# Other start addresses for the on-chip tiles of a convolution and feed-forward kernel

## The chip, the cores and the metric

The kernel runs on one core of a Trainium2 chip. The metric is the device time of one execution in microseconds (us): 2256.51 before the change, the median of 3 runs (2256.26 to 2256.53). The engines named below are TensorE (PE in the profile, with its weight loads as PEld), VectorE (DVE), ScalarE (ACT), GpSimd (POOL) and SyncE (SP, which here only issues transfers). SBUF is the on-chip memory of 128 partitions; an address below is a byte within a partition, the same one in all partitions. PSUM is the memory into which TensorE writes.

## The reference

A causal convolution of 7 taps, with softmax weights per head, feeds a two-layer network. x is [8, 4096, 192], the weights are w_in [192, 2048] and w_out [2048, 192], all in float32.

```python
w = exp(weight - max); w = w / (sum(w) + 1e-9)             # [8 heads, 7 taps]
x_unf = x_pad[:, idx, :].reshape(B, S, K, H, group)
conv = np.einsum('hk,bskhg->bshg', w, x_unf).reshape(B*S, D)
h = conv @ w_in
g = np.where(h >= 1, h, np.where(h <= -1, 0, (h + 1)**2 / 4))
out = g @ w_out
```

## The kernel before

**Tiling.** The 32768 tokens are cut into 64 blocks of 512, and the 2048 hidden columns into 16 chunks of 128, taken two at a time: 8 steps a block, 512 steps in all, each for one block `s` and one pair of chunks `j`. In a step, `mm1` computes the hidden values h of this step, and `mm2` adds the product of the values of two steps earlier to the sums of the output. Between the two, DVE clips h (L458), ACT squares (L464), DVE takes the maximum with h (L469), ACT rounds to a high part `gh` (L476), and DVE subtracts to get the low part `gl` (L482).

**Matmuls.** From the second block on, each factor is split into a high and a low part (type float32r), and three of the four products are computed. A matmul here takes 64 of the 128 rows of the array, and two of them, one on the upper and one on the lower 64 partitions, run side by side: a "pair" below. Each has 64x128 weights (one LDWEIGHTS) and a moving operand of 64x512 values, 2048 consecutive bytes in each partition. `mm1` (L407) is 9 such pairs in a step, with the weights from `W` (tile names w0 to w9) and the convolution's output (hi, lo, rh, rl, rhi, rlo) as the moving operand. `mm2` (L447) is 10 pairs, with weights from `W` and `WR` (wr) and gh or gl as the moving operand.

**The first block** is different: there `mm1` takes plain float32 (fp32) operands, with w_in's values `WI`, which lie in tiles of the names gh and gl, as weights, and the convolution's tiles as the moving operand. `mm2_first` (L425), for the first two blocks' sums, takes g as weights and `WF` (wf, 192 columns) as the moving operand. In the profile each fp32 matmul is recorded as two.

**Convolution.** For each two blocks, three tiles of x are loaded (raw), transposed on DVE (xT), multiplied by a tap's weight on ACT (p), and summed on GpSimd (y). Then y is split into hi and lo, and copies with the halves of the partitions exchanged are made by DMA (hi<-hi, lo<-lo and so on). `PLAN_A`, `PLAN_B` and `PLAN_R` set the step in which each part is issued; for example, the b tile is split in step 5 and first read by `mm1` in step 8. The very first unit of the convolution is summed on TensorE from xT (L190), with taps that start at `xT[.., SH + k]`, SH = 26 values.

**Order.** The schedule is written by hand (`manual_schedule`): each engine takes its instructions in the order of the program text, and each instruction waits on semaphores for what it reads.

**Addresses.** SBUF tiles are laid out from byte 16512 up, pool by pool in the order in which the pools are opened (L72 to L78), and within a pool in the order of first use; each tile takes its size rounded up to 32 bytes. Before the change that gives:

- const: W from 16512 (128 past a multiple of 1024), then WR, WF, wk, warm, whose, ident, up to 79680. W, WR and WF have sizes that are multiples of 512, and a matmul's 128 weights of 512 bytes start at multiples of 512 in them, so every weight load from them starts 128 past a multiple of 512.
- stage, 33792 bytes (33 times 1024).
- xin and xw (raw, xT, y, p), 21120 bytes, from 113472.
- xo, act, ob (hi, lo, rh, ..., gh, gl, g, sum, osb, t) from 134592. All of these tiles have 2048 or 4096 bytes, so all start 448 past a multiple of 1024, and 1472 past a multiple of 2048.

Of the kernel before, what the change touches and what calls it, by code (L numbers as in the profile page):

```python
# [8 lines left out]
F32 = mybir.dt.float32  # L9
# [9 lines left out]
P = 128  # L19
# [11 lines left out]
def lightconv_then_ffn(ctx: ExitStack, tc: tile.TileContext, x, weight, w_in, w_out, out):  # L31
# [26 lines left out]
    H, K = weight.shape  # L58
# [12 lines left out]

    const = ctx.enter_context(tc.tile_pool(name="const", bufs=1))  # L72
    stage = ctx.enter_context(tc.tile_pool(name="stage", bufs=2))
    xin = ctx.enter_context(tc.tile_pool(name="xin", bufs=3))
    xw = ctx.enter_context(tc.tile_pool(name="xw", bufs=2))
    xo = ctx.enter_context(tc.tile_pool(name="xo", bufs=3))
    act = ctx.enter_context(tc.tile_pool(name="act", bufs=2))
    ob = ctx.enter_context(tc.tile_pool(name="ob", bufs=2))  # L78
    ps_h = ctx.enter_context(tc.tile_pool(name="ps_h", bufs=2, space=PSUM))
    ps_o = ctx.enter_context(tc.tile_pool(name="ps_o", bufs=1, space=PSUM))  # L80
    ctx.enter_context(tc.manual_schedule())
# [53 lines left out]
    class Conv:  # L135
# [133 lines left out]
        def split_halves(self):  # L269
# [26 lines left out]
    wo_w = w_out.bitcast(U32).rearrange("(f p) (d two) -> p f d two", p=P, two=2)  # L296
    n_in = [CI if j < NPAIR else 0 for j in range(NCH)]
    n_all = [n_in[j] + (CO if j >= LAG else 0) for j in range(NCH)]
    W = [const.tile([P, 2, n_in[j] + (CW if j >= LAG else 0)], F32R, name=f"w{j}")
         for j in range(NCH)]  # L300
    CC = max(n_all)
# [12 lines left out]
    class Chunk:  # L314
# [51 lines left out]
        def parts(self, rest):  # L366
            j, k = self.j, n_in[self.j]
            if rest:
                yield (WF[j][:, :, 0:P],
                       *(W[j][:, i, k:].rearrange("p (f d) -> p f d", f=2) for i in range(2)))  # L370
                yield WF[j][:, :, P:], WR[j][:, :, 0], WR[j][:, :, 1]
            else:
                yield WI[j], W[j][:, 0, 0:k], W[j][:, 1, 0:k]

# [14 lines left out]
    def mm1(q):  # L389
# [11 lines left out]
        else:  # L401
            mms = [(W[j][:, part], u + u, [xop[s][u, x]] * 2) for u in "nsr"
                   for part, x in ((0, "hi"), (1, "hi"), (0, "lo"))]
# [25 lines left out]
    def mm2(q):  # L429

        s, j = divmod(q, NPAIR)
        gh, gl = ghs.pop(q), gls.pop(q)
        w, wr, k = W[j + LAG], WR[j + LAG], n_in[j + LAG]
        if j == 0:
# [97 lines left out]
    def evac_last(s):  # L532
# [29 lines left out]
                    in_=y[i][:, 0:2 * D].rearrange("p (b d) -> p b d", b=2))  # L562


    wk = const.tile([P, 2, K], F32, name="wk")
    warm = const.tile([P, 1], F32, name="warm")
    whose = const.tile([P, 2 * P + 3 * K + 3], F32, name="whose")[:, 0:2 * P]
    one = ob.tile([P, TB], F32, name="sum")[:, 0:P]
    small, busy = (ob.tile([P, TB // SQ, SQ], F32, name="osb").rearrange("p j b -> p (j b)")
                    for _ in range(2))  # L570
    wmax, wsum, wk2, rows = (small[:, i:i + n] for i, n in (
        (0, 1), (1, 1), (2, K), (2 + K, K)))
    ident = const.tile([P, P], F32, name="ident")


    KD = (("a", 0), ("r", 1), ("r", 3), ("r", 5), ("r", K - 1))
# [331 lines left out]
```

## Time and profile before

| | us |
|---|---|
| median of 3 runs (2256.26 to 2256.53) | 2256.51 |
| span of the profiled execution, first to last instruction | 2256.3 |
| ACT busy in it | 1697.6 (75%) |
| POOL busy in it | 1168.5 (52%) |
| DMA read from and written to HBM | 32.84 MB and 25.17 MB, 26 GB/s |

The profiled execution's own time is known by its span, and 2256.3 us lies within the three measured runs; nothing measurable stands around it. "Busy" of TensorE is the union of matmul durations, and these overlap, so a busy TensorE can still be waiting inside its pipeline; what tells is the distance from one matmul's start to the next. The chain of waits is followed back from the last instruction, at each step to what released it.

### The profile page before, as it was taken

The numbers are of one execution on the slowest core, as the hardware profiler recorded it, in microseconds if no ns is written. First come the engines' busy times: TensorE is split into PE (matmuls) and PEld (weight loads), VectorE is DVE, ScalarE is ACT, GpSimd is POOL, SyncE is SP. The second block draws the span as 40 slices with busy tenths as digits, with TensorE's granted clock in tenths as the row PEclk, the third lists the DMA queues.
The fourth block names the chain that finished last, engine by engine and source line by source line (L and its number), as shares of the span: only waits on it lengthen the run. The fifth ranks groups of instructions, "written<-read, shape, count | busy, mean of one in ns | idle before, by whom it ended". The sixth has DMA issues, their size and how long they took to land.

```text
span 2256.3 us, 48204 instructions
## 1 busy us (share of the span) xinstructions
PE 2250.8 (100%) x19646; PEld 2232.0 (99%) x19646; DVE 2103.4 (93%) x1883; ACT 1697.6 (75%) x2153; POOL 1168.5 (52%) x868
## 2 busy tenths in 40 slices
PE   9999999999999999999999999999999999999999
PEld 6999999999999999999999999999999999999999
DVE  8899999999999999999999999999999999999997
ACT  7677877778777787777877777877778777787775
POOL 1546644556445565454654455644556545565441
PEclk9999999999999999999999999999999999999999
DMA  7222222222222212222222222222222222212211
GB/s 158 49 51 46 43 44 49 51 52 39 52 48 46 53 35 51 49 49 51 39 47 47 49 51 49 40 48 45 50 53 39 51 49 46 54 34 51 49 34 24
DMA packets 442125, 110.84 MB, mean 49 GB/s; under 512 B 410288, under 2 KB 417840, under 8 KB 441904
## 3 DMA queue, kind: packets, MB, share of 16 engines
q1 hardware_dynamic: 441744, 107.66, 25.8%
q8 instruction: 155, 2.54, 0.5%
q14 instruction: 66, 0.54, 0.1%
q10 hardware_dynamic: 160, 0.10, 0.0%
HBM read 32.84 MB, written 25.17 MB: 26 GB/s over the span
## 4 chain that ended last, share of the span: by engine, by line
PE 100%; DMA 0%; DVE 0%; ACT 0%; issue 0%; DVEq 0%
PE h L407 47%; PE accm L447 30%; PE accr L447 20%; PE accr L425 1%; PE accm L425 1%; PE accr L190 0%; PE accr L407 0%; PE accm L175 0%; DMA osb<-in_weight_dram 0%; PE h L155 0%; PE accm L181 0%; PE accr L641 0%; PE h L548 0%; PE accm L407 0%; PE accr L548 0%
## 5 line engine op out<-in xcount | busy, mean ns | idle before, releaser
L230 POOL TENSOR_TENSOR y<-y,p 128x512 f32<-128x512 f32 x546 | 765.5, 1402 | 729.4 <-DVE g L469 558.6
L482 DVE TENSOR_TENSOR gl<-g,gh 128x1024 fp32r<-128x1024 f32 (+1 forms) x497 | 732.4, 1474 | 27.5 <-ACT gh L476 23.7
L407 PE MATMUL h<-hi,w 64*128 64x512 f32 x4032 | 740.6, 389 | 0.0
L464 ACT ACTIVATE g<-g 128x1024 f32<-128x1024 f32 (+1 forms) x505 | 535.2, 1060 | 241.8 <-DVE g L458 232.4
L476 ACT CAST gh<-g 128x1024 fp32r<-128x1024 f32 (+1 forms) x497 | 521.7, 1050 | 237.2 <-DVE g L469 223.6
L458 DVE TENSOR_SCALAR g<-h 128x1024 f32<-128x1024 f32 (+1 forms) x505 | 609.7, 1208 | 96.5 <-PE h L407 88.4
L469 DVE TENSOR_TENSOR g<-h,g 128x1024 f32<-128x1024 f32 (+1 forms) x505 | 613.6, 1215 | 11.9 <-ACT g L464 4.5
L447 PE MATMUL accm<-gh,w 64*128 64x512 f32 x3968 | 614.4, 388 | 0.0
L407 PEld LDWEIGHTS h<-hi,w 64*128 64x128 f32 x4032 | 580.3, 184 | 0.0
L407 PE MATMUL h<-lo,w 64*128 64x512 f32 x2016 | 555.9, 388 | 0.0
L447 PEld LDWEIGHTS accm<-gh,w 64*128 64x128 f32 x3968 | 513.1, 184 | 0.0
L447 PE MATMUL accr<-gh,wr 64*128 64x512 f32 x1984 | 387.3, 388 | 0.0
L447 PE MATMUL accm<-gl,w 64*128 64x512 f32 x1984 | 387.3, 388 | 0.0
L447 PE MATMUL accr<-gl,wr 64*128 64x512 f32 x1984 | 387.3, 388 | 0.0
L219 ACT ACTIVATE p<-xT,wk 128x512 f32<-128x512 f32 x562 | 375.0, 709 | 0.0
L407 PEld LDWEIGHTS h<-lo,w 64*128 64x128 f32 x2016 | 350.4, 184 | 0.4 <-DMA lo<-lo 0.2
L407 PE MATMUL h<-rhi,w 64*128 64x512 f32 x992 | 306.0, 388 | 0.0
L407 PE MATMUL h<-rh,w 64*128 64x512 f32 x992 | 306.0, 388 | 0.0
L447 PEld LDWEIGHTS accm<-gl,w 64*128 64x128 f32 x1984 | 286.1, 184 | 0.0
L447 PEld LDWEIGHTS accr<-gh,wr 64*128 64x128 f32 x1984 | 286.0, 184 | 0.0
L447 PEld LDWEIGHTS accr<-gl,wr 64*128 64x128 f32 x1984 | 286.0, 184 | 0.0
L496 POOL TENSOR_TENSOR sum<-t 128x512 f32<-128x512 f32 (+1 forms) x124 | 160.7, 1317 | 127.0 <-ACT t L494 127.0
(143 smaller groups left out, 1975.3 us busy)
## 6 DMA issues: line engine op xcount, KB each, us to landing
out_dram<-osb SPq DMA_DIRECT2D x366, 64.0 KB, 2.0
raw<-in_x_dram SPq DMA_DIRECT2D x334, 68.0 KB, 2.4
hi<-hi SPq DMA_DIRECT2D x126, 128.0 KB, 2.3
lo<-lo SPq DMA_DIRECT2D x126, 128.0 KB, 2.4
rhi<-rh SPq DMA_DIRECT2D x62, 128.0 KB, 2.2
rlo<-rl SPq DMA_DIRECT2D x62, 128.0 KB, 2.3
words<-in_moe_w_in_dram SPq DMA_DIRECT2D x16, 192.0 KB, 3.9
words<-in_moe_w_out_dram SPq DMA_DIRECT2D x8, 384.0 KB, 4.6
```

The lines of the kernel that those rows point to most:

```text
L219: nc.scalar.mul(p, self.xT[:, SH + k:SH + k + TB], wk[:, self.wsel, k:k + 1])
L230: nc.gpsimd.tensor_add(y, y, self.product(k))
L407: nc.tensor.matmul(h[e], w[HALVES[e], c0:c0 + P], x[e][e], start=(n == 0), stop=(n == len(mms) - 1))
L425: nc.tensor.matmul(accs[s][a, i][:, c0:c0 + D], g[half, e, b * P:(b + 1) * P], w[half, e, :], start=(j == 0 and e == 0 and b % 2 == 0), st ...
L447: nc.tensor.matmul(accs[s][a, i], st, g[HALVES[i], e, :], start=(j == 0 and n == first[a]), stop=(j == NPAIR - 1 and n == last[a]))
L458: nc.vector.tensor_scalar(out=g[:, e, :], in0=hs[q][:, e, :], scalar1=-1.0, scalar2=1.0, op0=ALU.max, op1=ALU.min)
L464: nc.scalar.activation(g[:, e, :], g[:, e, :], AF.Square, bias=0.5, scale=0.5)
L469: nc.vector.tensor_tensor(out=g[:, e, :], in0=h[:, e, :], in1=g[:, e, :], op=ALU.max)
L476: nc.scalar.copy(gh[:, e, :], gs[q][:, e, :])
L482: eng.tensor_sub(gl[:, e, :], g[:, e, :], gh[:, e, :])
L496: nc.gpsimd.tensor_add(y[:, n], t[0][:, n], t[1][:, n])
```

## The change

No instruction, no wait and no size of an operand changes, and the list of instructions of each engine is the same before and after, with the waits in it. What changes are the start addresses in SBUF.

```diff
     stage = ctx.enter_context(tc.tile_pool(name="stage", bufs=2))
-    xin = ctx.enter_context(tc.tile_pool(name="xin", bufs=3))
-    xw = ctx.enter_context(tc.tile_pool(name="xw", bufs=2))
     xo = ctx.enter_context(tc.tile_pool(name="xo", bufs=3))
     act = ctx.enter_context(tc.tile_pool(name="act", bufs=2))
     ob = ctx.enter_context(tc.tile_pool(name="ob", bufs=2))
+    xin = ctx.enter_context(tc.tile_pool(name="xin", bufs=3))
+    xw = ctx.enter_context(tc.tile_pool(name="xw", bufs=2))
...
+    wk = const.tile([P, 2, K], F32, name="wk")
+    warm = const.tile([P, 1], F32, name="warm")
+    whose = const.tile([P, 2 * P + 72], F32, name="whose")[:, 0:2 * P]
+    ident = const.tile([P, P], F32, name="ident")
     W = [const.tile([P, 2, n_in[j] + (CW if j >= LAG else 0)], F32R, name=f"w{j}")
          for j in range(NCH)]
...
-    wk = const.tile([P, 2, K], F32, name="wk")
-    warm = const.tile([P, 1], F32, name="warm")
-    whose = const.tile([P, 2 * P + 3 * K + 3], F32, name="whose")[:, 0:2 * P]
     one = ob.tile([P, TB], F32, name="sum")[:, 0:P]
...
-    ident = const.tile([P, P], F32, name="ident")
```

The four small tiles now come first: wk at 16512, warm, whose with a longer pad, and ident at 17920. They end at 18432, which is 18 times 1024. The other tiles follow from there:

| tiles | before | after |
|---|---|---|
| W | 16512, 128 past a multiple of 1024 | 18432, a multiple of 1024 |
| weight loads from W, WR, WF | 128 past a multiple of 512 | multiples of 512 |
| words, m, r, wa (stage) | 832 past a multiple of 1024 | multiples of 1024 |
| hi, lo, ..., gh, gl, g, sum, osb, t | 448 past a multiple of 1024 | multiples of 1024 |
| raw (three buffers) | 832, 960 and 64 past | 0, 128 and 256 past |
| xT (two) | 192 and 320 past | 384 and 512 past |
| y and p | 448 past | 640 past |

Before and after, every tile of matmul operands starts at a multiple of 64 bytes. The start of a weight load and the start of the moving operand of the same matmul stand 320 bytes apart, counted modulo 512, before the change, and 0 after.

## The prediction

> **What bounds the kernel now.** I read the page's busy times first, then the chain that ended last.
>
> ```profile
> PE 2250.8 (100%) x19646; PEld 2232.0 (99%) x19646; DVE 2103.4 (93%) x1883; ACT 1697.6 (75%) x2153; POOL 1168.5 (52%) x868
> PE 100%; DMA 0%; DVE 0%; ACT 0%; issue 0%; DVEq 0%
> ```
>
> TensorE is the whole chain. A busy share of 100% only says that matmuls overlap, so next comes what its weight loads (which go ahead of the matmuls) waited for, in the view of waits: us in total, times, longest.
>
> ```profile
> PEld h L407 <- issue: 7.1, 32, 0.2
> PEld accm L425 <- issue: 2.2, 10, 0.2
> PEld h L407 <- DMA lo<-lo: 0.2, 1, 0.2
> ```
>
> These are the largest for TensorE's main loops, and the only wait for a DMA is 0.2 us. The kernel waits for nobody; its time is a number of matmuls times the distance between their starts. The chain in order of time gives that distance (start us, length us, pieces):
>
> ```profile
> 102.26 2.06 PE h L407 x18
> 104.32 1.37 PE accm L447 x12
> 105.69 0.91 PE accr L447 x8
> 106.61 2.06 PE h L407 x18
> ...
> 2241.91 2.06 PE h L407 x18
> ```
>
> A step is 18 + 12 + 8 matmuls, so 19 pairs. From the first `mm1` shown to the last lie 2139.65 us; at 4.35 us a step (106.61 - 102.26) that is 492 steps, 4.3489 us each, and divided by 19 it is **228.9 ns a pair**. The windows show that it is the same everywhere, at full granted clock (the first of the columns after POOL is the clock):
>
> ```profile
> 102.26:345.79 243.53, 243.53 (x2131) 243.53 (x2130) 227.48 (x195) 187.06 (x236) 136.65 (x98) 1.00 0.24 45
> 1200.00:2240.00 1040.00, 1040.00 (x9092) 1040.00 (x9090) 975.97 (x835) 782.39 (x973) 542.75 (x388) 1.00 0.25 45
> ```
>
> **The sum.** `mm1` has 9 pairs in the 504 steps after the first block, `mm2` 10 pairs in the 496 steps after the second: 4536 + 4960 = 9496 pairs, times 228.9 ns = 2173.6 us. The other 82.7 us of the span are the start, the fp32 matmuls of the first blocks, and the end. So 1 ns on a pair is 9.5 us, and 0.2% of the time (4.5 us, about what a measurement of this kernel can tell from no change) is 0.47 ns on a pair. The question is only whether new addresses move 228.9 ns by half a nanosecond.
>
> **What is in the 228.9 ns.** The fp32 stage of the same trace shows what an undisturbed stream costs:
>
> ```profile
> 16.84 5.15 PE h L407 x24
> ...
> 32.57 0.65 PE accm L425 x8
> 33.22 0.65 PE accr L425 x8
> 33.87 0.65 PE accm L425 x8
> 34.52 0.65 PE accr L425 x8
> ```
>
> Twelve pairs of 512 columns in 5.15 us are 429 ns each; four pairs of 192 columns in 0.65 us are 162.5 ns each. The difference, 266.5 ns over 320 columns, is 0.833 ns a column, and 2.5 ns are left as a fixed cost per pair. If float32r streams at exactly twice that rate, which is an estimate, a pair should take 213.3 + 2.5 = 215.8 ns. It takes 228.9. **13.1 ns a pair, 124 us in all, are not explained by the columns**, and they are what an address could reach.
>
> The Trainium skill, "TensorE: Matmul & The Clock Gate", section "Back-to-back issue gap", gives N / 2.4 + 2.5 ns for an isolated warm matmul, 215.8 ns for 512 columns: the estimate above. By that rule the float32r stage would be 9496 x 13.1 ns = 124 us shorter than the trace has it. The trace decides for the kernel as it is.
>
> **Part 1: weights from 128 to 0, moving operands from 448 to 0 (modulo 512 and 1024).** Three rows speak on whether a start address matters.
>
> First, the fp32 stage already mixes phases. WI lies in gh and gl tiles, so its weight loads and the moving hi tiles both start 448 past a multiple of 512: 0 apart, what the change makes everywhere. In L425 the weights (g) start at 448, and the moving wf starts at 128 or 640 for the first of its two halves and at 896 or 384 for the second (its row is 768 bytes), modulo 1024. All these come out at the same 0.833 ns a column and 2.5 ns; the four rows at 32.57 to 34.52 span both halves, 0.65 us each.
>
> Second, the taps of the first convolution unit start at 4 x (26 + k) bytes in xT, 108, 116 and 124 for k = 1, 3, 5, not even multiples of 16:
>
> ```profile
> 10.39 1.88 PE L190 MATMUL accr<-xT,t 128*128 128x512 f32 x4
> L190 PE MATMUL accr<-xT,t 64*128 64x512 f32 x2 | 1.0, 589 | 0.0
> ```
>
> The timeline's four matmuls take 1.88 us, less the last one's own 0.589, so three starts in 1.29 us, 430 ns each, against 429 for aligned operands.
>
> Third, within float32r the weight loads start at 128 and at 640 modulo 1024 (c0 and the two parts of W are multiples of 512), and every matmul of hi, whatever chunk it meets, has nearly one duration (ns, min/median/max):
>
> ```profile
> L407 PE MATMUL h<-hi,w x3936: 385/388/392, 101.9 to 2238.3; 64*128 64x512 f32 x197
> ```
>
> Against all that: the first two are at half the column rate, where reads have slack, and no float32r row has its moving operand anywhere but at 448. So the trace doesn't show the exact case. The cost is bounded from both sides: at best all of the 13.1 ns goes (-124 us), at worst it doubles (+124 us); the nearest rows, the spread of 385 to 392 around 388, bound a small effect at about 3 ns a pair, 28 us either way. I take **0**, since the rows nearest in kind (429 and 430 ns, at phases 0 apart and off every line) agree on it.
>
> **Part 2: raw, xT, y, p and the transfers.** Transfers into and out of moved tiles land in 2.2 to 2.4 us:
>
> ```profile
> raw<-in_x_dram SPq DMA_DIRECT2D x334, 68.0 KB, 2.4
> hi<-hi SPq DMA_DIRECT2D x126, 128.0 KB, 2.3
> ```
>
> raw is loaded 4 steps (17.4 us) before its transpose, and the exchanged halves are written 3 steps (13.0 us) before `mm1` reads them, so a gain or a loss of tenths of a us is hidden by the matmuls of those steps. With that cover gone, half a us late on each of 31 double blocks would cost some 15 us. I take 0. DVE, ACT and POOL read the same tiles from new addresses; DVE is the closest to the bound, with 2256.3 - 2103.4 = 152.9 us idle. g, gh and gl all move by the same number of bytes, so nothing changes between the operands of its three costly instructions. I take 0 here as well.
>
> **Part 3: start and end.** These are a chain of single waits, where an address could show at once:
>
> ```profile
> 0.80 1.95 DMA osb<-in_weight_dram
> 14.18 0.51 PE accm L407
> 2250.04 0.38 ACT t L541
> ```
>
> About 14 us lie ahead of the first `mm1` and 6 us behind the last sum. Two transfers stand in them; landings here differ by 0.4 us between kinds, so I allow 0.8 us either way and take 0. The sum is 2256.3 + 0 for the profiled execution. The median of the three runs lies 0.2 above it, so I predict **2256.5 us**.
>
> **Rivals.**
>
> *The pair gets shorter.* If reads of moving operands and weights disturb each other or cross a boundary more often from 448 than from 0, part of the 13.1 ns goes. For it: the 13.1 ns exists, and exists only where columns go twice as fast. Against it: the fp32 rows, and the equal 388 at weights of 128 and 640. Price: 3 ns give 2256.5 - 28 = 2228 us, all of it gives 2132 us. It counts from 0.47 ns on.
>
> *The pair gets longer.* Weight load and moving operand of a matmul now start at the same place modulo 512, and the load runs while the previous matmul on its rows streams, from tiles at the same phase too:
>
> ```profile
> L447 PEld LDWEIGHTS accm<-gh,w 64*128 64x128 f32 x3968 | 513.1, 184 | 0.0
> ```
>
> For 184 ns of 228.9 both read the same partitions. If memory is interleaved by these low address bits, an equal phase means more collisions than 320 bytes apart. 3 ns more give 2285 us; doubling the 13.1 gives 2381. It decides from 0.47 ns. Against it: the stage with both at 448 has none of it, though at half rate. The Trainium skill, in the same page's section "Step-by-step: what each phase is for", says that TensorE has two independent SBUF read ports, one for the moving operand and one for LDWEIGHTS, so that a load takes nothing from a running matmul; by that rule both rivals on the pair fall, and the sum stays at 2256.5. No row here can show ports.
>
> *DVE becomes the bound.* Its subtraction has a long tail beside GpSimd's additions:
>
> ```profile
> L482 DVE TENSOR_TENSOR gl<-g,gh x492: 1197/1252/2292, 101.1 to 2236.4; 128x1024 fp32r<-128x1024 f32 x164
> L482 DVE TENSOR_TENSOR gl<-g,gh 128x1024 fp32r<-128x1024 f32 x495 | 731.1, 1477 | 27.1 <-ACT gh L476 23.2
> ```
>
> If y and p, now at another phase than g, made each of 495 meet GpSimd more often, it would have to rise by 152.9 / 495 = 0.31 us on the mean of 1477 ns before it costs anything; at the maximum of 2292 on all, 403 - 153 = 250 us, 2507. Nothing ties that wait to an address.
>
> **How the numbers follow.** No change: 0.62, 2254 to 2259 by part 3 and half a ns. Shorter pair: 0.21, of which 0.12 lie within 3 ns (down to 2228) and 0.09 beyond. Longer pair: 0.14, of which 0.09 lie within 3 ns (up to 2285) and 0.05 beyond. DVE: 0.03, above 2285. The range 2228 to 2285 leaves out 0.09 + 0.05 + 0.03 = 0.17. Faster 0.21, same 0.62, slower 0.17.
>
> **What would show it.** Right: the chain's `mm1` pieces still come every 4.349 us, 2.06 + 1.37 + 0.91, and the median of hi's matmuls stays at 388 ns. A shorter or longer pair shows in just these rows, evenly over the whole span. DVE as the bound would show as TensorE waiting for gl (L482) in the view of waits. Wrong would be any pitch off 228.9 ns by more than 0.5, or a gap that opens in front of `mm1` because a transfer came late.

## The result, and the profile after

The changed kernel takes 2235.2 us (median of 4 runs, 2234.93 to 2235.57) against 2256.39 before (2256.09 to 2256.53). The ratio is 0.9907, with a 95% interval from 0.9893 to 0.9921: 21.2 us, 0.9%, faster. "No change" had the highest chance in the prediction, so its likeliest case did not come. It was the first rival that came, a shorter pair. One execution of the kernel before, beside e11 and e12 below, took 8072.78 us against a median of 2256.29, and the ratios leave it out.

The page of after, engines' busy times, and the chain in order of time (start us, length us, pieces; L411 is the old L407, L451 the old L447):

```profile
PE 2227.3 (100%) x19646; PEld 1850.7 (83%) x19646; DVE 2093.3 (94%) x1883; ACT 1693.7 (76%) x2153; POOL 1173.8 (53%) x868
```

```profile
104.40 2.04 PE h L411 x18
106.44 1.36 PE accm L451 x12
107.80 0.91 PE accr L451 x8
108.70 2.04 PE h L411 x18
...
2219.02 2.04 PE h L411 x18
```

TensorE is still the whole chain; only the pieces have become shorter, `mm1` from 2.06 to 2.04 us. From 104.40 to 2219.02 lie 491 steps of 19 pairs, so a pair takes 226.67 ns where it took 228.89. Times 9496 pairs that is 21.1 us, the whole of the measured 21.2.

The profiled spans differ by more, 2256.3 to 2233.2, 23.1 us. The other 1.9 us are the start of the one execution profiled before the change: its first `mm1` came at 14.0 us, while after it came at 12.1 us, with faster small matmuls ahead of it:

```profile
4.11 0.41 PE accr L641 x2
4.51 0.46 PE h L155 x4
```

Before, the same two pieces took 0.66 and 0.85 us. The clock records of the traces go with this: full clock is granted from 9.96 us on in the one execution profiled before, and from some time between 4.0 and 6.9 us in all eleven other profiled executions of this kernel and its variants, whose first `mm1` comes at 11.95 to 12.60 us, e4 below with the old pair among them (12.6). So the start does not belong to the change. From the first `mm1` to the last instruction the two traces differ by 21.2 us (2242.3 and 2221.1).

A span is also not the whole time of an execution: where both are known the time is 1.7 us longer (2234.93 us for the span of 2233.2 above). The execution profiled before thus took about 2258 us, an estimate, and lies above the measured runs, not within them. Its span is longer than those of the other executions of that kernel near 2256 us, which are 2254.0 to 2255.2.

Nothing that TensorE waits for moved. Its waits are the same few (7.0 us at `mm1`, in 32 pieces, and 2.2 at `mm2_first`), and the transfers land as before:

```profile
PEld h L411 <- issue: 7.0, 32, 0.2
PEld accm L429 <- issue: 2.2, 10, 0.2
```

```profile
raw<-in_x_dram SPq DMA_DIRECT2D x334, 68.0 KB, 2.4
hi<-hi SPq DMA_DIRECT2D x126, 128.0 KB, 2.3
```

The fp32 pairs of the first blocks did not move either. `mm2_first` (now L429) went from a distance of 192 bytes, counted modulo 256, between its weights and its moving operand to 0, and its pieces take the same 0.65 us as before:

```profile
14.95 5.15 PE h L411 x24
30.67 0.65 PE accm L429 x8
```

One more number changed: PEld's share fell from 99% to 83%. Before, the lower half's matmul started 163 ns behind the upper half's of the same pair. After, it started 223 ns behind it, and so 3 to 4 ns ahead of the upper half's next one, so that the weight loads of both halves lie on top of each other. (The 3 ns that the expectations below give as the lag after the change are this distance to the next pair.) That this lag is the cause had to be a rival too (theory S).

### The profile page after: what moved, and what is told of

It reads as the page before. It is cut to its first block, busy times and chain, and to the rows that moved or that the text cites. A ratio compares the mean times of both kernels' runs of the same rounds, so it can differ in the third digit from the quotient of the medians.

```text
span 2233.2 us, 48204 instructions
## 1 busy us (share of the span) xinstructions
PE 2227.3 (100%) x19646; PEld 1850.7 (83%) x19646; DVE 2093.3 (94%) x1883; ACT 1693.7 (76%) x2153; POOL 1173.8 (53%) x868
## 4 chain that ended last, share of the span: by engine, by line
PE 99%; ACT 0%; DMA 0%; DVE 0%; issue 0%; DVEq 0%; ACTq 0%
PE h L411 47%; PE accm L451 30%; PE accr L451 20%; PE accr L429 1%; PE accm L429 1%; PE accr L190 0%; PE accr L411 0%; DMA osb<-in_weight_dram 0%; PE accm L181 0%; PE h L552 0%; ACT xT L168 0%; ACT xT L165 0%; ACT xT L167 0%; PE accm L411 0%; PE h L155 0%
## 5 line engine op out<-in xcount | busy, mean ns | idle before, releaser
L230 POOL TENSOR_TENSOR y<-y,p 128x512 f32<-128x512 f32 x546 | 798.2, 1462 | 733.3 <-DVE g L473 560.7
L411 PE MATMUL h<-hi,w 64*128 64x512 f32 x4032 | 764.7, 387 | 0.0
L451 PE MATMUL accm<-gh,w 64*128 64x512 f32 x3968 | 639.6, 387 | 0.0
L411 PEld LDWEIGHTS h<-hi,w 64*128 64x128 f32 x4032 | 561.3, 185 | 75.4
L411 PE MATMUL h<-lo,w 64*128 64x512 f32 x2016 | 613.0, 387 | 0.0
L451 PEld LDWEIGHTS accm<-gh,w 64*128 64x128 f32 x3968 | 463.6, 184 | 75.6
L451 PE MATMUL accr<-gh,wr 64*128 64x512 f32 x1984 | 414.8, 387 | 0.0
L451 PE MATMUL accr<-gl,wr 64*128 64x512 f32 x1984 | 414.8, 386 | 0.0
L451 PE MATMUL accm<-gl,w 64*128 64x512 f32 x1984 | 414.7, 387 | 0.0
L411 PEld LDWEIGHTS h<-lo,w 64*128 64x128 f32 x2016 | 371.3, 184 | 38.1 <-DMA lo<-lo 0.2
L451 PEld LDWEIGHTS accm<-gl,w 64*128 64x128 f32 x1984 | 276.4, 184 | 37.9
L451 PEld LDWEIGHTS accr<-gh,wr 64*128 64x128 f32 x1984 | 276.3, 184 | 37.8
L451 PEld LDWEIGHTS accr<-gl,wr 64*128 64x128 f32 x1984 | 276.2, 184 | 37.9
L411 PE MATMUL h<-rhi,w 64*128 64x512 f32 x992 | 304.1, 386 | 0.0
L411 PE MATMUL h<-rh,w 64*128 64x512 f32 x992 | 304.1, 386 | 0.0
```

The costliest lines, as they stand in the source:

```text
L230: nc.gpsimd.tensor_add(y, y, self.product(k))
L411: nc.tensor.matmul(h[e], w[HALVES[e], c0:c0 + P], x[e][e], start=(n == 0), stop=(n == len(mms) - 1))
L451: nc.tensor.matmul(accs[s][a, i], st, g[HALVES[i], e, :], start=(j == 0 and n == first[a]), stop=(j == NPAIR - 1 and n == last[a]))
```

## The experiments

All but e8, e11 and the two programs e9 and e10 use the changed kernel's text with small tiles or pools in other places, so that only addresses change; e8 and e11 do the same to the text before. "Distance" is the start of the moving operand less the start of the weight load, in bytes; pair times are worked out from the first and last steps as above. e1, e2, e11 and e12 were executed four or five times, the others once, and there the pair time in the trace carries the reading.

**e1: weights as after, moving operands as before.**

```diff
+    xin = ctx.enter_context(tc.tile_pool(name="xin", bufs=3))
     xo = ctx.enter_context(tc.tile_pool(name="xo", bufs=3))
...
-    ident = const.tile([P, P], F32, name="ident")
     W = [...]
...
+    ident = const.tile([P, P + 16], F32, name="ident")[:, 0:P]
```

> Weights as after the change (multiples of 512), moving operands as before it (448 past a multiple of 1024). Theory W, the start of the weight load decides: 226.7 ns a pair, about 2235 us. Theory M, the start of the moving operand decides: 228.9 ns a pair, about 2256 us. Theory D, the distance between the two starts modulo 512 decides, and only a distance of 0 is fast: it is 448 here, so 228.9 ns. Theory S, the lag of the lower half's matmuls behind the upper half's decides (163 ns before, 3 ns after, set by chance of timing), whatever the addresses: the pair follows the lag that this run has, 228.9 at 163, 226.7 at 3.

**e2: moving operands as after, weights as before** (wk, warm, whose and ident stand behind WF).

```diff
-    wk, warm, whose, ident
     W = [...]
...
+    wk, warm, whose, ident
```

> Moving operands as after the change (multiples of 1024), weights as before it (128 past a multiple of 512). Theory M: 226.7 ns a pair, about 2235 us. Theory W: 228.9 ns, about 2256 us. Theory D: the distance is 384, so 228.9 ns. Theory S: the pair follows the lag of this run.

**e3: a distance of 0 with nothing aligned** (e2 with 32 more values of pad in whose).

> Weights 128 past a multiple of 512 and moving operands 128 past a multiple of 1024: a distance of 0, with neither aligned. Theory D: 226.7 ns a pair, about 2235 us. Theories M and W: 228.9 ns, about 2256 us. Theory S: the pair follows the lag of this run.

**e4: weights at multiples of 512, moving operands 64 further** (ident behind WF with a pad of 16 values, pools as after).

> Weights at multiples of 512, moving operands 64 past a multiple of 1024. Theory W: 226.7 ns a pair, about 2235 us. Theory M with an edge of 128 bytes or more: 228.9 ns, about 2256 us. Theory D: the distance is 64, so 228.9 ns. Theory S: the pair follows the lag of this run.

Measured: e1 2298.3 us (ratio 1.0186, 1.0169 to 1.0203), e2 2289.0 us (1.0145, 1.013 to 1.016), e3 2234.95 us and e4 2256.34 us. Each half of the change alone makes the kernel slower than before, and e3 has the whole gain with weights and moving operands of the main loop at no more than a multiple of 128 bytes. Theories M and W fall. Of D it holds that the distance decides and that 0 is fast; its 228.9 ns for every other distance does not, since e1 takes 233.3 and e2 232.4, which no theory had. The steps of e1 and of e3, in the chain:

```profile
1000.99 2.10 PE h L411 x18
1003.09 1.40 PE accm L451 x12
1004.49 0.93 PE accr L451 x8
1005.42 2.10 PE h L411 x18
```

```profile
1000.10 2.04 PE h L411 x18
1002.14 1.36 PE accm L451 x12
1003.50 0.91 PE accr L451 x8
1004.40 2.04 PE h L411 x18
```

4.43 us a step in e1, 4.30 in e3: each piece is longer by the same share, `mm1` and `mm2` alike. Theory S falls by the busy times of e3 and of e4:

```profile
PE 2227.2 (100%) x19646; PEld 2206.5 (99%) x19646; DVE 2093.7 (94%) x1883; ACT 1693.8 (76%) x2153; POOL 1174.2 (53%) x868
```

```profile
PE 2249.2 (100%) x19646; PEld 1903.7 (84%) x19646; DVE 2103.9 (93%) x1883; ACT 1697.4 (75%) x2153; POOL 1168.4 (52%) x868
```

e3 is fast with the loads spread over 99% of the span (a lag of 77 ns), e4 is slow with them on top of each other (84%, 10 ns). e6 below has the lag of the kernel before, 163 ns, and another pair time. In all twelve traces of the kernel and its variants the lag is the same at 150 and at 2200 us, and two executions of one program have different lags (223 ns after, 210 in e12), at the same pair time.

**e5, e6, e7: three more distances** (256, 32 and 480; ident behind WF with a pad of 64, 8 and 24 values; e7 with xin ahead of xo).

> Distance of the moving operand's start from the weight load's, modulo 512: 256. So far the pair took 226.7 ns at 0 (twice), 228.9 at 64 and at 320, 232.4 at 384 and 233.3 at 448. Theory D256, the memory repeats every 256 bytes: 226.7 ns, about 2235 us. Theory D512, it repeats every 512 bytes and 64 and 320 agree by chance: a value between 228.9 and 233, 2256 to 2298 us.

> Distance 32, with tiles at odd multiples of 32 bytes. If the cost climbs evenly from 0 to 64: 227.8 ns a pair, about 2246 us. If only whole 64-byte units count: 226.7 or 228.9 ns. If a start at an odd multiple of 32 costs of itself: above 228.9 ns, over 2256 us.

> Distance 480 modulo 512, 224 modulo 256. If the cost goes on climbing up to the next repeat: 234 ns or a little more a pair, about 2303 us. If it falls back evenly from 192 to 256: about 230 ns, 2267 us. If the best place lies just under the repeat: below 226.7 ns, under 2235 us.

| kernel | weights mod 512 | moving mod 1024 | distance mod 256 | ns a pair | us |
|---|---|---|---|---|---|
| after | 0 | 0 | 0 | 226.67 | 2235.2 |
| e3 | 128 | 128 | 0 | 226.67 | 2234.95 |
| e5 | 0 | 256 | 0 | 226.67 | 2235.44 |
| before | 128 | 448 | 64 | 228.89 | 2256.39 |
| e4 | 0 | 64 | 64 | 228.89 | 2256.34 |
| e2 | 128 | 0 | 128 | 232.37 | 2289.0 |
| e1 | 0 | 448 | 192 | 233.33 | 2298.3 |
| e6 | 0 | 32 | 32 | 233.33 | 2298.38 |
| e7 | 0 | 480 | 224 | 233.33 | 2298.46 |

e5's steps, in the chain:

```profile
1000.76 2.04 PE h L411 x18
...
1005.07 2.04 PE h L411 x18
```

So these distances repeat every 256 bytes (D256; D512 would have put e5 above 228.9), and the time neither climbs evenly nor falls back: all three guesses for e7 and the first two for e6 were wrong. The third one for e6, that an odd multiple of 32 costs of itself, has the right sign; but e8 has all its operands of W at 480 and the moving ones at odd multiples of 32 too, and those pairs take 226.67.

**e8: only the weights of WR at another distance** (both x pools ahead; wk, warm and 32 bytes of pad between W and WR).

```diff
+    whose = const.tile([P, 2 * P + 88], F32, name="whose")[:, 0:2 * P]
     W = [...]
+    wk = const.tile([P, 2, K], F32, name="wk")
+    warm = const.tile([P, 1 + 8], F32, name="warm")[:, 0:1]
     WR = [...]
     WF = [...]
+    ident = const.tile([P, P + 64], F32, name="ident")[:, 0:P]
```

> Distance 0 for all matmuls with weights from W, 384 for the 4 of 19 pairs of a step with weights from WR alone (wr). Theory L, a weight load disturbs the matmul that is running while it reads: 15 pairs at 226.7 and 4 at about 232.4 ns, 227.9 on average, about 2246 us, and the four longer gaps lie one pair early, before the wr matmuls start. Rival O, a matmul is slow by the distance between its own two operands: the same sum, but the longer gaps follow the wr matmuls' own starts. If the distance acts only through the tiles' common layout: one even pitch.

2255.06 us, 228.77 ns a pair on average. The time from one start to the next on the same half, averaged from 150 to 2150 us of the trace, where each of the six long gaps stands 920 times:

```
from          to            ns
gl,w          gl,w          226.67
gl,w (last)   gh,wr         232.50
gh,wr         gh,wr         240.83
gh,wr         gl,wr         232.50
gl,wr         gl,wr         230.83
gl,wr (last)  hi,w          232.50
hi,w          hi,w (next)   230.83
all others                  226.67
```

The first long gap lies before any wr matmul has started, while a matmul with weights from W at distance 0 runs and the first wr weights are loaded. That is where theory L has it: the load disturbs the stream that is running. Rival O, which would have had the first long gap at the first wr matmul itself, falls. A variant of O has not been tested by addresses: that a wr matmul's own distance delays its own start, which would put these gaps in the same places. What speaks against it is the order in time. The first wr load is recorded with 184 ns, as other loads, and at 1003 us it ends 45 ns before the wr matmul starts, so that matmul does not wait for a longer load. L also expected four gaps and 2246 us, and there are six: the last two come after the last wr load. How a disturbed matmul hands this on is not settled. The six together are 40 ns longer than six of 226.67.

**e9: many distances by themselves.** A program with TensorE alone, 40 pairs a stretch:

```python
for r in range(n):
    for i, half in enumerate(halves):
        c, d = w0 + P * (r % 8), m0 + step * (r % 3)
        nc.tensor.matmul(acc[2 * (r % 2) + i], w[half, c:c + P], m[half, d:d + TB],
                         start=True, stop=True)
```

> A program of its own, which computes none of the reference's output: stretches of 40 float32r pairs like the kernel's, all with TensorE alone, each stretch with one distance between the moving operand and the weight load. Names: m is the moving operand's shift in bytes with the weights fixed, w the weights' shift, both a shift of both, full a 128-row matmul in place of the pair, bf the same in bfloat16. If the distance modulo 256 alone decides: 226.7 ns a pair at 0 and 256, 228.9 at 64 and 320, 232.4 at 128 and 384, 233.3 at 32, 192, 224 and 448, the same for both64 and both192 as for 0, and w64, w128, w192 like m192, m128, m64. If the kernel's other engines have a part in it: other values here. If some distance lets the load pass the stream without a collision: a pair below 226.7 ns, at the least 215.8 by the fp32 stage's fixed 2.5 ns. Rows of 16 bytes as the unit: m4, m8 and m12 like m0 or m16.

The chain gives each stretch's length for 80 matmuls, without the DVE, ACT or GpSimd work of the kernel:

```profile
54.60 9.47 PE m64x L62 x80
...
83.35 9.36 PE m112x L62 x80
92.75 9.61 PE m128x L62 x80
...
131.43 9.62 PE m192x L62 x80
...
160.30 9.74 PE m240x L62 x80
...
170.08 9.38 PE m256x L62 x80
...
189.02 9.58 PE m384x L62 x80
...
208.30 9.83 PE m4x L62 x80
...
275.60 9.39 PE both64x L62 x80
...
285.04 9.39 PE both192x L62 x80
...
294.47 18.44 PE full0x L62 x80
312.95 18.61 PE full64x L62 x80
...
350.60 18.95 PE full192x L62 x80
369.58 17.44 PE bf0x L62 x80
387.07 17.44 PE bf64x L62 x80
...
422.03 17.43 PE bf192x L62 x80
```

Between starts on one half, from the eleventh of a stretch on: 226.7 ns at 256, 228.9 at 64 and 320, 233.4 at 32, 233.3 at 192 and 224, 226.7 for both192 and both64, all as in the kernel, and 232.2 at 384 as in e2. So the other engines have no part in it, and moving both operands together changes nothing. But the distance modulo 256 alone does not decide: 128 takes 233.5 ns (233.4 with 128 rows, here and in e10), while 384 takes 232.2, and 232.4 in w128 and in e2, whose distance is 384 too. These two are told apart only modulo 512. Nor is it a smooth curve: 231.5 ns at 16, 230.0 at 208, 236.8 at 240. Steps of 4 bytes count too (238.6 at 4, 233.3 at 8, 228.9 at 12), so rows of 16 bytes are not the unit. The best found is 226.7, at 0 and again at 112; none of the 24 distances tried lies below. The 128-row matmul behaves like the pair (226.7, 228.9, 233.3 ns at 0, 64 and 192). bfloat16 takes 215.8 ns at every distance tried. The first stretch (m0) says nothing on distances: the trace's clock record has full clock from 19.1 us on, and up to there its starts are 427 ns apart.

**e10: narrower weights and shorter streams**, the same program with 128-row matmuls.

> A program of its own, which computes none of the reference's output: stretches of 80 128-row float32r matmuls with TensorE alone. In a name c is the number of weight columns, n that of moving columns, m the distance in bytes; start is the first stretch, twice, while the clock comes up. Theory L, the load of the next weights takes cycles from the running stream, one per 16 bytes of weights at distance 0: c128 takes 512 + 32 cycles (226.7 ns), c96 512 + 24 (223.3), c64 512 + 16 (220.0), c32 at most 217; with 384 and 256 moving columns the same 32 cycles stand over a shorter stream, 173.3 and 120.0 ns. Rival F, a fixed cost of a float32r matmul: 226.7 ns for all four widths at distance 0, and the distance matters as much for narrow weights. bf: 215.8 ns at both widths.

```profile
53.19 18.48 PE c128n512m0x L61 x80
...
128.35 18.66 PE c96n512m0x L61 x80
...
203.42 18.63 PE c64n512m0x L61 x80
...
278.16 18.73 PE c32n512m0x L61 x80
...
353.16 14.18 PE c128n384m0x L61 x80
...
395.87 9.86 PE c128n256m0x L61 x80
...
415.52 9.36 PE c128n256m192x L61 x80
```

Both theories fail on the widths: 226.7, 230.0, 230.1 and 231.7 ns for 128, 96, 64 and 32 columns at distance 0. At this distance fewer weights are not cheaper, so the cost is not one cycle per 16 bytes loaded, and it is not the same fixed cost at all widths either. The distance matters less for narrow weights: from 64 bytes to 192 it moves a matmul from 228.4 to 232.6 ns at 64 columns, and at 32 columns the four distances lie within 1.2 ns, where at 128 they spread over 6.7. The shorter streams came as L had it, 173.3 and 120.0 ns at distance 0; but with 256 columns the best distance is another one, 113.3 ns at 192. What the best distance is depends on the shape. bfloat16 takes 215.8 ns with 64 columns too.

**e11: the smallest edit for the gain**, the kernel before with wk ahead of W, and **e12**, the changed kernel on the same chip.

```diff
+    wk = const.tile([P, 2, K], F32, name="wk")
     W = [const.tile([P, 2, n_in[j] + (CW if j >= LAG else 0)], F32R, name=f"w{j}")
...
-    wk = const.tile([P, 2, K], F32, name="wk")
     warm = const.tile([P, 1], F32, name="warm")
```

> The kernel before with one tile moved: wk, 64 bytes, ahead of W. Weight loads start 192 past a multiple of 512, moving operands stay 448 past a multiple of 1024, so the distance is 256, which is 0 modulo 256; nothing starts at a multiple of 128. Distance theory: 226.7 ns a pair, about 2235 us, the whole gain of the change. If the alignment itself matters: 228.9 ns, about 2256 us.

> The changed kernel again, on the same chip as the one with wk ahead of W. Distance theory: both take the same time, about 2235 us, within 0.1%.

e11 takes 2235.21 us and e12 2234.99 us, both 0.9907 of before (0.9893 to 0.9921). Moving 64 bytes of constants gives the whole gain, with neither weights nor moving operands of the main loop at a multiple of 128. No kernel here beats the changed one by more than 0.3 us.

## Why the prediction came out as it did

*What bounds the kernel* was right: TensorE alone, 19 pairs a step, 9.5 us for each ns on a pair. The result is just that product, 2.22 ns times 9496. That 13.1 ns of the pair were not explained by the columns also held; 2.2 of them went, inside the bound of 3 ns taken from the spread of durations. That the time lay within the range is partly luck: the likeliest case had a term of 0, and other addresses of the same kind (e1, e6, e7) give 2298 us, beyond the range's upper end.

*Part 1 failed at "I take 0".* By the sign that the prediction named itself, a pitch more than 0.5 ns off 228.9, this term was wrong: the pitch is 226.67 ns over the whole span. It rested on three rows. The first could not tell: 0.833 ns a column and 2.5 ns were worked out from the `mm1` row and the `mm2_first` row alone, and two numbers fitted to two rows always agree with them; also, the four starts named for `mm2_first` are all the same distance, 192 modulo 256. That fp32 pairs do not depend on the distance is shown by the second row, and by `mm2_first` before and after the change. But the effect is one of float32r, and neither fp32 nor bfloat16 shows it here; the text named this gap and then took the rows nearest in kind anyway. The third row, hi's matmuls at weights of 128 and 640, could not have shown anything: these two are the same modulo 512, so the distance is the same. All float32r matmuls of the kernel before stand at one distance, 320 modulo 512, so its trace could not say what another distance costs.

It did hold a hint. Before, the gaps on one half take turns at about 226, 229 and 232 ns, which is also why hi's durations spread from 385 to 392 ns. After, the gaps are 225 to 228 ns and the durations nearly equal:

```profile
L411 PE MATMUL h<-hi,w x3924: 385/387/387, 104.1 to 2214.8; 64*128 64x512 f32 x197
```

Matmuls of one shape that come unevenly, with nobody to wait for, point at something other than columns and a fixed cost.

*The first rival* had the right sign, and 2.2 ns lie within its 3. It gave two reasons. That moving operands and weights disturb each other is what the runs bear out; that an aligned start crosses fewer boundaries is wrong: e1 and e2 align one operand each and lose 42 and 33 us, e3 and e11 align neither and gain. *The second rival* had the right quantity, the distance between weight load and running stream, and the wrong sign: an equal phase is the best here, not the worst. Which sign it has, nothing on record before the change could tell.

The Trainium skill, "TensorE: Matmul & The Clock Gate", section "Step-by-step: what each phase is for", has weight loads take nothing from a running matmul. e8 speaks against it for float32r: while the first load at a bad distance is read, the next start comes 5.8 ns later (232.50 for 226.67). By the formula of the Trainium skill, same page, section "Back-to-back issue gap", N / 2.4 + 2.5 ns, 512 columns take 215.8 ns; the bfloat16 stretches of e9 take 215.8, and no float32r stretch does.

*Parts 2 and 3* were right: transfers, DVE and GpSimd show no change that TensorE waits for, and nothing of start or end is due to the change. DVE did not become the bound.

## What to carry to other kernels

When TensorE is saturated, compare the distance between matmul starts with the columns it streams; what is left over can depend on addresses although no instruction waits. For float32r, on this chip, look at the start of the moving operand less that of the weight load, modulo 512: put all pairs at the same good distance (0 or 256 for 512 columns and 128 weights), and change pads of other tiles only with that in view, since 64 bytes ahead of the weights are worth 21 us here and a half-done alignment loses 33 or 42. A rate that every matmul of a trace shares can't be judged from that trace; a short program that sweeps the one suspected number settles it in one run.

## What was not expected of the hardware

- A float32r matmul of 512 columns and 128 weight columns takes 226.7 to 238.6 ns depending on the distance alone, while bfloat16 takes 215.8 at each of four distances.
- Many averages fall on steps. In units of 0.4167 ns, half the 0.833 ns that a column takes in the fp32 stage, 226.67 ns is 544, 233.33 is 560, 173.33 is 416 and 113.33 is 272, all multiples of 16, and three of 228.89 make 1648, also a multiple. Single gaps do not: those of 226, 229 and 232 ns in the kernel before, and 230.0 ns (552) on average at 208 bytes, are no such multiples. So it is not that each start falls on a step of 16, and what the steps are stays open. Why 112 bytes is as good as 0, and why narrower weights are slower at a distance of 0, stays open too.
- The lag between the two halves' matmuls differs from run to run (10 to 223 ns), stays the same from 150 to 2200 us, and costs nothing: 226.67 ns was measured at lags of 77, 137, 210 and 223 ns.
